# Chunk 0's 2 KB rows of q and k, dealt to partitions by sixteenth of the chunk instead of by head

## The chip, the core and the metric

The kernel runs on one core of a Trainium2 chip. The metric is device time in microseconds (us) of one execution: 240.31 us, the median of three runs from 240.06 to 241.03. The execution that was profiled took 239.83 us.

## What is computed

A retention layer with a recurrent state per head, followed by a gated feed-forward layer. Sizes: 4 batches, 8 heads, 768 positions, head width 64; feed-forward width 1536.

```python
gamma = 1.0 - 2.0 ** (-5.0 - np.arange(H))
for t in range(S):
    state = gamma * state + np.einsum('bhd,bhe->bhde', k[:, :, t], v[:, :, t])
    y[:, :, t] = np.einsum('bhd,bhde->bhe', q[:, :, t], state) / np.sqrt(D)
x = y.transpose(0, 2, 1, 3).reshape(B * S, H * D)
xn = x / np.sqrt(np.mean(x * x, -1, keepdims=True) + 1e-6) * rms_g
g = xn @ w_gate
out = (g / (1 + np.exp(-g)) * (xn @ w_val)) @ w_out
```

All inputs and the output are float32 in HBM, q, k and v laid out as batch, head, position, width.

## The kernel before, in words

The recurrence is computed by chunks: 768 positions are 6 chunks (c) of 128, and each chunk has 4 batches (b). For one (c, b) the steps are: load q, k and v; make them bfloat16; turn q and k so that the width is on partitions (`qT`, `kT`); scores `a = kT qT` for all heads (L382); scores times a decay mask (`am`, L405); `y = am v`, plus the state's part for c > 0 (L420, L424); mean square (`S`, L448, ScalarE), its inverse root (`R`, L458 and L460, GpSimd), normalised rows `xn` (`N`, L472, VectorE), turned to `xnT`; and the update of the state (`K`, `U`, `B`). Then the feed-forward layer for the 512 rows of a chunk: `g` and `v` matmuls over 12 blocks of the width (L538), SiLU (`s`, L548), product (`h`, L556), and the matmul with `w_out` (`d`, L563).

The order of all work is written out by hand in the string `ORDER`: each word is one step, done by one function, and each engine executes its own instructions in that order. A word such as `Lk.0.2@S>iota` reads: load k, chunk 0, batch 2, issued by SyncE (S), after the step `iota`. `Tk.0.3/5` is the turning of k of batch 3 on TensorE into PSUM bank 5; `Ek.0.3@D` is the copy of that bank to SBUF on VectorE; `Ck.0.2@D` is a cast to bfloat16 on VectorE. `H.14` and `hot.3` are matmuls on a tile of ones whose result nobody reads.

Chunk 0's q and k are loaded in a way of their own. A row of the load is 8 consecutive positions of one head, 8 x 64 float32 = 2 KB. There are 8 heads x 16 groups of 8 positions = 128 such rows, one for each partition. The access pattern is made on L139, and the load is issued on L291:

```python
by8 = {n: x.rearrange("b h (c s j) d -> c b h s (j d)", s=C // NJ, j=NJ)[0] for n, x in (("q", q), ("k", k))}
i = done[n, c, b] = e.dma_start(out=flat(x), in_=by8[n][b])
```

So partition 16 h + s holds positions 8 s to 8 s + 7 of head h. Three of these eight loads (k of batches 0, 3 and 2, in this order) are issued by SyncE in float32 and cast on chip (`Ck`). Five (q of batches 2 and 1, k of batch 1, q of batches 0 and 3, in this order) are issued by GpSimd, which lets the transfer write bfloat16: 2 KB rows are read and 1 KB rows written. All other loads of q, k and v have a partition per position, with 256-byte runs of the heads (L293).

`T` turns a loaded tile: for each of the 8 positions j of a row and each parity i of the head it makes one matmul of the tile's slice (128 partitions x 64) with 64 columns of the identity matrix, picked by `pick` (L345) so that the columns are head pair, then group s. In this kernel these columns are 4 runs of 16 neighbouring columns. That is 16 matmuls for one tile. `E` copies the bank to SBUF and puts the positions in order.

VectorE's order at the start is: constants, `Ck.0.2`, `Ck.0.3`, then the copies `Eq.0.2`, `Ek.0.3`, `Ek.0.2`, `Eq.0.0`, then `D.0.2` (L506) and the masked scores (L405). TensorE's is: `H.14`, `Tk.0.3`, `Tq.0.2`, `hot.3`, `Tq.0.1`, `Tk.0.2`, `Tk.0.0`, `H.1`, `Tq.0.0`, `Tk.0.1`, then the scores. GpSimd issues, in order, the five loads above, v of batches 0, 2 and 1, k of chunk 1 batch 1, `wv` columns 0 to 255, v of batch 3, three loads of `wg` and one of `wv`, and k of chunk 1 batch 0; its ninth and later loads each wait until the load eight before has landed. Only after them in its queue come the `R` steps and then the next weight load, `wv.4.6`.

Of the kernel before, what the change touches and what calls it, by code (L numbers as in the profile page):

```python
# [103 lines left out]
def kernel(  # L104
# [15 lines left out]
    C = 128  # L120
    NCH = S // C
    NHP = H // 2
# [13 lines left out]
    rows = {n: s.rearrange("b h (c p) d -> b c p h d", p=C) for n, s in (("q", q), ("k", k), ("v", v))}  # L136

    NJ = 8
    by8 = {n: x.rearrange("b h (c s j) d -> c b h s (j d)", s=C // NJ, j=NJ)[0] for n, x in (("q", q), ("k", k))}  # L139

    DVE, ACT, POOL, SP = nc.vector, nc.scalar, nc.gpsimd, nc.sync
    ENG = {"D": DVE, "A": ACT, "P": POOL, "S": SP}
# [5 lines left out]
    def flat(x):  # L148
        return x.rearrange("p h d -> p (h d)")
# [24 lines left out]
    ident = const.tile([128, 128], BF16, name="ident")  # L174
# [22 lines left out]
    def bank(i, shape, dtype, name):  # L197
        return psum.tile(shape, dtype, name=name, tag=f"bank{i}")
# [142 lines left out]
    def T(n, bk, c, b):  # L341
        u = t[c, b]
        if c == 0:
            u[n + "P"] = p = bank(bk[0], [128, NHP, NJ, C // NJ], F32, "t_ps")
            pick = ident.rearrange("p (hp i s) -> p i hp s", i=2, hp=NHP)  # L345
            for j in range(NJ):
                for i in range(2):
                    nc.tensor.matmul(p[i * 64:i * 64 + 64, :, j, :], u[n + "b"][:, j, :], pick[:, i],  # L348
                                     start=True, stop=True)
            return  # L350
        u[n + "P"] = bank(bk[0], [128, NHP, 128], BF16, "t_ps")
        for hp in range(NHP):
            nc.tensor.transpose(u[n + "P"][:, hp, :], flat(u[n + "b"])[:, hp * 128:(hp + 1) * 128], ident)  # L353
# [14 lines left out]
    for n in "qk":  # L368
        F["T" + n] = lambda e, bk, c, b, n=n: T(n, bk, c, b)
        F["E" + n] = lambda e, bk, c, b, n=n: E(n, e, c, b)  # L370
        F["t" + n] = lambda e, bk, c, b, n=n: tr(n, c, b)
# [253 lines left out]
```

## Time and profile before

| what | value |
|---|---|
| profiled execution | 239.83 us |
| its span, first to last instruction | 238.1 us |
| outside the span | 1.7 us |
| TensorE busy | 225.5 us, 95% of the span |
| VectorE, ScalarE, GpSimd busy | 55%, 41%, 38% |
| mean granted TensorE clock | 0.993 |
| DMA over the span | 34.27 MB, mean 144 GB/s |
| the three k loads by SyncE issued | 0.79 to 2.9 us |
| the five 2 KB-row loads by GpSimd issued | 2.08 to 5.23 us |
| first cast of a loaded tile on VectorE | 10.35 us |

The profile gives, among others: the busy share of each engine in slices of the span; the chain of work that ended last, followed back from the last instruction, with its releasers; the waits; the instructions in order of time; and, for chosen stretches, busy time, the granted TensorE clock, the DMA share (mean number of packets in flight per DMA engine, of 16) and the rate. The trace also has a record of each DMA packet (start, length, bytes) and of each count that a load adds to its semaphore when a part of it has landed; a load has landed with the sixteenth count.

### The profile page before, as it was taken

How to read it: one execution, taken by the hardware profiler on the slowest of the kernel's cores; microseconds unless marked ns; L12 is line 12 of the kernel's file. 1: busy time of each engine (PE TensorE's matmuls, PEld its weight loads, DVE VectorE, ACT ScalarE, POOL GpSimd, SP SyncE). 2: the span in 40 equal slices, each digit the busy share in tenths (PEclk: the TensorE clock that was granted, in tenths of full speed). 3: DMA queues.
4: the chain of work that ended last, by engine and by line, in shares of the span. 5: the costliest groups of instructions: out<-in, count | busy, mean ns of one | idle time of the engine just before them, and what ended most of it. 6: DMA issues, size and time to landing. Idle time of an engine off the chain costs nothing.

```text
span 238.1 us, 4684 instructions
## 1 busy us (share of the span) xinstructions
PE 225.5 (95%) x1782; PEld 121.0 (51%) x1807; DVE 131.2 (55%) x234; ACT 97.1 (41%) x234; POOL 90.3 (38%) x164
## 2 busy tenths in 40 slices
PE   8099999999989999999999999999999999999995
PEld 2066785545544466544554445545454444444453
DVE  3179647874686769445575428693675441432300
ACT  6158565633444274064432044423176321233021
POOL 8584898271350615426137242266504000000000
PEclk9979999999999999999999999999999999999999
DMA  3999599999948796799999999899503302001123
GB/s 99 182 159 161 55 178 220 206 201 214 194 94 188 155 225 145 174 227 191 203 237 179 197 222 181 170 214 149 150 3 82 75 23 78 10 0 44 48 106 116
DMA packets 101233, 34.27 MB, mean 144 GB/s; under 512 B 89945, under 2 KB 97625, under 8 KB 101210
## 3 DMA queue, kind: packets, MB, share of 16 engines
q1 hardware_dynamic: 80186, 25.97, 54.4%
q0 software_dynamic: 21024, 8.00, 27.4%
q8 instruction: 14, 0.23, 0.4%
q14 instruction: 9, 0.07, 0.1%
HBM read 28.31 MB, written 6.29 MB: 145 GB/s over the span
## 4 chain that ended last, share of the span: by engine, by line
PE 84%; DVE 5%; DMA 3%; POOL 3%; issue 2%; ACT 1%; SPq 1%; POOLq 0%; ACTq 0%
PE o_ps L563 25%; PE v_ps L538 24%; PE g_ps L538 23%; DMA kf<-in_k_dram 3%; PE a_ps L382 2%; PE kv_ps L515 2%; PE y_ps L420 2%; DVE am L405 2%; PE y_ps L424 1%; PE t_ps L348 1%; PE o_ps L585 1%; POOL rstd L460 1%; PE t_ps L353 1%; DVE kb L146 1%; PE xt_ps L485 1%
## 5 line engine op out<-in xcount | busy, mean ns | idle before, releaser
L556 DVE TENSOR_TENSOR hT<-sg,v_ps 128x512 bf16<-128x512 bf16 (+2 forms) x76 | 48.0, 656 | 51.5 <-PE v_ps L538 34.1
L538 PE MATMUL v_ps<-xnT,wv_b 128*128 128x512 bf16 (+2 forms) x335 | 71.3, 343 | 1.3 <-DVE hT L556 1.0
L538 PE MATMUL g_ps<-xnT,wg_b 128*128 128x512 bf16 (+2 forms) x337 | 70.9, 344 | 0.5 <-issue 0.2
L548 ACT ACTIVATE sg<-g_ps 128x512 bf16<-128x512 f32 (+2 forms) x76 | 42.1, 574 | 66.3 <-PE g_ps L538 64.3
L563 PE MATMUL o_ps<-wo_b,hT 128*128 128x512 bf16 x267 | 62.2, 379 | 0.5
L538 PEld LDWEIGHTS <-wv_b 128*128 128x128 bf16 x344 | 30.2, 98 | 29.1 <-issue 1.2
L538 PEld LDWEIGHTS <-wg_b 128*128 128x128 bf16 x344 | 30.3, 98 | 28.7
L563 PEld LDWEIGHTS <-hT 128*128 128x128 bf16 x276 | 26.2, 98 | 29.3 <-DVE hT L556 0.3
L405 DVE TENSOR_TENSOR am<-a_ps,causal 128x512 bf16<-128x512 f32 x40 | 25.7, 684 | 7.0 <-PE a_ps L382 7.0
L320 POOL TENSOR_TENSOR qb<-qf,ydec 128x512 bf16<-128x512 f32 x13 | 14.2, 1093 | 24.2 <-DMA qf<-in_q_dram 24.2
L146 ACT COPY o_sb<-o_ps 128x512 f32<-128x512 f32 (+2 forms) x17 | 9.2, 549 | 34.2 <-PE o_ps L563 32.7
L530 POOL CAST st_b<-st_f 64x256 bf16<-64x256 f32 x40 | 17.6, 440 | 8.6 <-PE y_ps L424 4.6
L146 DVE COPY o_sb<-o_ps 128x512 f32<-128x512 f32 (+1 forms) x9 | 5.8, 650 | 22.4 <-PE o_ps L563 12.3
L458 POOL TENSOR_SCALAR ms<-ssq 128x1 f32<-128x1 f32 x24 | 4.6, 192 | 31.1 <-ACT xsq L448 30.2
L460 POOL TENSOR_TENSOR rstd<-ms,mhalf 128x1 f32<-128x1 f32 x24 | 13.6, 567 | 2.0
L448 ACT ACTIVATE xsq<-y_ps 128x512 f32<-128x512 f32 x14 | 8.4, 598 | 10.7 <-PE y_ps L424 9.2
L523 DVE TENSOR_TENSOR st_f<-st_f,kv_ps 128x512 f32<-128x512 f32 x16 | 10.7, 682 | 3.3 <-POOL st_b L530 2.0
L472 DVE SCALAR_TENSOR_TENSOR xn<-y_ps,rstd,g_bc 128x512 bf16<-128x512 f32 x14 | 10.4, 747 | 1.8 <-POOL rstd L460 1.6
L337 ACT ACTIVATE vp<-vf,vdec 128x64 bf16<-128x64 f32 x40 | 10.1, 338 | 1.3 <-DMA vf<-in_v_dram 1.3
L339 POOL TENSOR_TENSOR vp<-vf,vdec 128x512 bf16<-128x512 f32 x8 | 8.8, 1100 | 3.3 <-DMA vf<-in_v_dram 3.2
L231 PE MATMUL hot_ps<-one 128*128 128x512 bf16 x23 | 7.6, 472 | 1.1 <-DVE one L153 1.1
L420 PEld LDWEIGHTS <-am 128*128 128x128 bf16 x144 | 6.4, 98 | 4.0 <-DVE am L405 1.0
(97 smaller groups left out, 187.3 us busy)
## 6 DMA issues: line engine op xcount, KB each, us to landing
out_dram<-o_sb SPq DMA_DIRECT2D x23, 256.0 KB, 2.6
kf<-in_k_dram SPq DMA_DIRECT2D x19, 256.0 KB, 4.4
qf<-in_q_dram SPq DMA_DIRECT2D x16, 256.0 KB, 3.7
vf<-in_v_dram SPq DMA_DIRECT2D x16, 256.0 KB, 4.0
wo_b<-in_moe_w_out_dram POOLq DMA_DIRECT2D x3, 512.0 KB, 13.0
qb<-in_q_dram POOLq DMA_DIRECT2D x8, 128.0 KB, 7.2
vf<-in_v_dram POOLq DMA_DIRECT2D x4, 256.0 KB, 8.5
wv_b<-in_moe_w_val_dram POOLq DMA_DIRECT2D x3, 256.0 KB, 6.1
```

The costliest lines, as they stand in the source:

```text
L146: (e.copy if e is ACT else e.tensor_copy)(out, in_)
L320: e.tensor_tensor(out=u["qb"], in0=u["qf"], in1=ydec[:, c, :, None].to_broadcast([128, H, D]), op=ALU.mult)
L405: DVE.tensor_tensor(out=u["am"][:, i], in0=u["a"][i], in1=m, op=ALU.mult)
L420: nc.tensor.matmul(y[:, h, :], u["am"][:, h % 2, h // 2, :], u["vp"][:, h, :], start=h == 0, stop=c == 0 and h == H - 1, skip_group_check= ...
L460: POOL.tensor_tensor(out=u["rstd"], in0=ms, in1=mhalf, op=ALU.pow)
L472: DVE.scalar_tensor_tensor(out=u["xn"], in0=flat(u.get("x", u["y"])), scalar=u["rstd"], in1=g_bc, op0=ALU.mult, op1=ALU.mult)
L523: DVE.tensor_tensor(out=st_f[b], in0=st_f[b], in1=t[c, b]["kv"], op=ALU.add)
L530: POOL.tensor_copy(st_b[b][r, :, i * 64:i * 64 + 64], st_f[b][r, :, i * 64:i * 64 + 64])
L538: nc.tensor.matmul(p[:, (n - n0) * m:(n - n0 + 1) * m], W[w][0][:, s, n * 128:(n + 1) * 128], xnT[c][:, s, b0 * C:b1 * C], start=s == 0, s ...
L548: ACT.activation(sg[:, :cols], done["wg", c, n0, b0][:, :cols], AF.Silu)
L556: DVE.tensor_tensor(out=hT[c][:, n0:n1, b0 * C:b1 * C], in0=sg, in1=p, op=ALU.mult)
L563: nc.tensor.matmul(o_ps[c, b], hT[c][:, n, b * C:(b + 1) * C], wo_b[:, n, :], start=n == 0, stop=n == NFF - 1)
```

## The change

The sixteenth of the chunk, s, becomes the outer dimension of the DRAM side of these eight loads, and the head the inner one. Partition 8 s + h then holds positions 8 s to 8 s + 7 of head h. Rows are 2 KB as before and there are 128 of them; neighbouring partitions now read rows one head apart, 768 x 64 x 4 bytes = 192 KB, where they read neighbouring rows before. `pick` follows: its 64 columns are now single columns, 8 apart, in place of runs of 16.

```diff
-    by8 = {n: x.rearrange("b h (c s j) d -> c b h s (j d)", s=C // NJ, j=NJ)[0] for n, x in (("q", q), ("k", k))}
+    by8 = {n: x.rearrange("b h (c s j) d -> c b s h (j d)", s=C // NJ, j=NJ)[0] for n, x in (("q", q), ("k", k))}
...
-            pick = ident.rearrange("p (hp i s) -> p i hp s", i=2, hp=NHP)
+            pick = ident.rearrange("p (s hp i) -> p i hp s", i=2, hp=NHP)
```

The instructions of every engine, their number and their order are the same in both kernels.

## Prediction

> **What bounds the kernel.** I read the page first: TensorE is busy 95% of the span, so time can only be saved where it is not. The 40 slices of busy tenths show where: the second (6 to 12 us) has a 0, all others but the last have 8 or 9.
>
> ```profile
> PE   8099999999989999999999999999999999999995
> ...
> PEclk9979999999999999999999999999999999999999
> ```
>
> Right behind it, in the third slice, the granted clock is 0.7, the only one below 0.9. Next the chain that ended last, in order of time.
>
> ```profile
> 2.29 8.03 DMA kf<-in_k_dram
> 10.32 0.02 issue
> 10.35 1.16 DVE kb L146 x2
> 11.50 0.04 issue
> 11.55 1.07 PE t_ps L348 x32
> ...
> 14.94 0.39 PE t_ps L348 x16
> 15.33 0.02 issue
> 15.35 0.60 DVE qT L146
> 15.95 0.05 issue
> 16.00 0.69 DVE kd L506
> 16.70 2.99 DVE am L405 x5
> ```
>
> The end hangs on a transfer: SyncE's third k load (batch 2) lands at 10.32 us; then two casts, the turning of q and k, and VectorE's queue, which is busy without a gap over 0.4 us from 15.35 (`Eq.0.0`) to 24.8 us. From there to the end the chain is almost all TensorE: no DMA stands in it again. So a microsecond won before 15.35 is a microsecond won at the end, unless a transfer becomes late behind it.
>
> Then the stretches around these loads (the last columns are granted clock, DMA share of 16 engines, GB/s).
>
> ```profile
> 2.50:3.50 1.00, 1.00 (x4) 0.32 (x3) 0.74 (x3) 0.99 (x2) 1.00 (x2) 1.00 0.37 102
> 3.50:4.50 1.00, 1.00 (x4) 0.30 (x3) 0.00 (x0) 1.00 (x4) 1.00 (x3) 1.00 0.59 203
> 5.50:7.00 1.50, 0.46 (x3) 0.00 (x0) 0.00 (x0) 1.24 (x5) 1.50 (x2) 1.00 1.01 186
> 18.00:21.00 3.00, 2.94 (x54) 1.94 (x55) 3.00 (x6) 2.13 (x6) 0.96 (x3) 1.00 1.45 196
> 24.00:27.00 3.00, 2.83 (x45) 2.40 (x42) 1.99 (x6) 1.45 (x4) 2.02 (x6) 1.00 0.00 0
> ```
>
> While only SyncE's loads move (3.5 to 4.5), the share is about a half. By the packet records 50 packets of 2 KB start in each half microsecond and each takes 84 ns: 50 x 84 / 500 = 8.4 in flight. The counts say the same: eight of a load's sixteen come at once (first load: by 1.95 us, before its first packet at 2.30), eight with the data (4.44 to 4.91). Loads with 128 rows outermost (v of batch 0) bring all sixteen with their data. So a load whose DRAM side has 8 as outer dimension is worked by eight engines, 16 packets each. GpSimd's loads are also dealt to eight, and by their counts alternate between the two halves: q.0.2, k.0.1 and q.0.3 share the half of SyncE's three loads, and land at 10.11, 11.25 and 12.62.
>
> **The change: transfers.** With 16 as outer dimension I take it that each load runs on sixteen engines, 8 packets each. SyncE's three loads are then 24 packets per engine in place of 48. Of them 3 go in the slow first 0.7 us (26 packets on eight engines from 2.3 to 3.0 in the record), 21 at 84 ns = 1.76: last packet done at 2.3 + 0.7 + 1.76 = 4.76. GpSimd's first load joins at 4.0 to 4.9 and may put 3 of its packets (98 ns) between: 5.1. The last count came 0.35 to 0.8 us behind the first load's last packet: I take 0.4. Landing 5.5, not 10.32: **-4.8 us**.
>
> GpSimd's issues stay at 2.08 to 5.23 (0.6 each). Its loads now need 8 x 98 ns = 0.8 us each. From about 4.9: q.0.2 lands at 6.2, q.0.1 7.0, k.0.1 7.7, q.0.0 8.5, q.0.3 9.3; then v of batches 0, 2, 1, at 0.85 apart as in the counts of before: 10.2, 11.0, 11.9 (13.49, 14.33, 15.17 before). Its ninth load waits for q.0.2's landing (2.4 us of idle, at 10.39); that is gone, since q.0.2 lands while it still issues (to 7.97). The nine loads from k.1.1 to k.1.0 took 9.2 us after v.0.1 (15.17 to 24.39): now to about 21.
>
> **The change: the turning.** From VectorE's first cast to `Eq.0.0` it was 15.35 - 10.35 = 5.0 us: 1.2 for the casts, 3.8 for six tiles' turning, of which 3.2 at clock 0.50. TensorE then had been idle from 5.96 to 11.54. Now the casts end at 6.7 and it is idle for 0.7 us, so I take the full clock. A tile's 16 matmuls then take 0.27 (14.87 to 15.14) in place of 0.44 (11.55 to 11.99):
>
> ```profile
> 11.55 0.64 PE L348 MATMUL t_ps<-ident,kb 128*64 128x64 bf16 x16 [5.59 <-DVE kb L146]
> 11.99 0.62 PE L348 MATMUL t_ps<-ident,qb 128*64 128x64 bf16 x16
> ...
> 14.87 0.44 PE L348 MATMUL t_ps<-ident,qb 128*64 128x64 bf16 x16
> 15.14 0.42 PE L348 MATMUL t_ps<-ident,kb 128*64 128x64 bf16 x16
> ```
>
> Six tiles (1.65) and the two blocks of filler matmuls (0.55) end at 6.7 + 2.2, with 0.15 until the copy; VectorE's three copies before `Eq.0.0` (0.6 each) begin 0.7 after the first tile: 6.7 + 0.7 + 1.8 = 9.2. Both give `Eq.0.0` at about 9.2, 3.7 after the first cast: **-1.3 us**. Sum -6.1.
>
> The new `pick` reads single columns 8 apart. No row before reads a moving tile with gaps. Bounds: 0 (the rows above, same matmul, nearest), and 2.5 times a tile's time, from the farthest matmul row, float32 columns (L275, two in 1.12 us, 0.56 each against 0.22 for 512 bfloat16 columns): 6 x (0.68 - 0.27), about +2.4. A gain has no source. I take +0.1, near the first: its copies leave little cover.
>
> **What is late next.** Needed against landing, after: q.0.1 7.5 against 7.0; q.0.0 8.75 against 8.5; v.0.2 (first y, 2.6 after `Eq.0.0`) 11.8 against 11.0; the first `wg` (23.9 before, 17.8 now) against 16.2. All hold, q.0.0 barely. The next weight load stands behind GpSimd's `R` of batch 3, so its issue (25.80) moves with the chain to 19.7 and its packets (27.4) to 21.3, just when k.1.0's are through: the empty 24 to 27 us shown above is used up, and more than about -6.1 would not be followed by the weights. These are nearly late already: `wg.6.9`, `wv.6.9` and `wg.9.12` land 1.0, 0.6 and 0.8 us before their first use at 36.6, 39.9 and 42.9. So a chain that gains 6.0 has weights that gain about 6.0, and the slack stays.
>
> **Forecast:** 239.83 - 6.0 = 233.8 for a profiled execution; the median of the runs is 0.5 above that execution: 234.3, and 232.9 to 235.0 for this case. Chance 0.60.
>
> **Rivals.**
> (a) Transfers scale less than I take, or GpSimd's q.0.0 arrives late and TensorE waits. The fastest half microsecond with 2 KB packets in it (6.5 to 7.0) moved 230 GB/s; at that rate 786 KB take 3.4 us, the landing is at 6.8, gain 4.8: 235.5. For it: no row has sixteen engines on 2 KB packets. Against: 18 to 21 us wrote 196 GB/s in bfloat16, which is 390 read. 0.16.
> (b) The gapped columns cost. At twice the time per tile (0.54) six tiles and the fillers take 3.8, and `Eq.0.0` is at 10.65, 1.5 later: gain 4.6, 235.7; at 2.5 times (0.68) it is 2.3 later: 236.5. [...] No run here shows it yet. 0.13.
> (c) The loads stay on eight engines: 240.3. Against it are the sixteen counts with data of loads with 128 outermost. [...] 0.05.
> (d) Slower: each engine now jumps 192 KB from row to row. If a jump cost what the first ten packets did (336 ns against 84), the 56 packets per engine up to q.0.0 would take 18.8 us: landing 2.5 + 18.8 + 0.4 = 21.7. q.0.0 may land at 14.9 without loss (`Eq.0.0` at 15.35), so 6.8 are lost: 247. It decides from 0.21 us per packet. Against it: eight engines on eight heads, 192 KB apart, already run at 84 ns. 0.06.
>
> **How the numbers follow.** Faster by over 0.5% (1.2 us, about what a measurement of this kernel can tell): forecast, (a) and (b), 0.89; within: (c), 0.05; slower: (d), 0.06. The range reaches from the forecast's lower end to a microsecond past (b)'s upper end, for (a) and (b) together: 233.0 to 237.5; it leaves out (c), (d) and a little of the forecast.
>
> **What would show it.** The third k load landing near 5.5 with a DMA share near 1 by 3.5 to 4.5; all sixteen counts with data; VectorE's first cast near 5.5, `Eq.0.0` near 9.2; clock 1.0 through the turning, 16 matmuls in 0.27; GpSimd without the 2.4 us wait; `wv.4.6` issued near 19.7; no weight wait of TensorE at 30 to 37 us. Wrong if packets grow well over 100 ns, if a tile's turning takes over 0.4 at full clock, or if the chain after 24 us shows a DMA.

## The result and the profile after

The changed kernel is slower, by less than a per cent: 242.77 us (median of 14 runs, 240.65 to 245.46) against 240.65 us (14 runs, 240.06 to 241.31). The ratio is 1.007, 95% interval 1.0044 to 1.0096; the three slowest runs of the changed kernel, with a mean granted clock of 0.965, are left out of it. The prediction was 234.3 us, range 233.0 to 237.5. The profiled execution took 241.65 us, its span 239.9, 1.8 more than before.

The busy slices of the page, of the changed kernel. The idle stretch of the second slice (the 0 before) is a 5 now: TensorE starts earlier. But the granted clock, the last row, is lower there (6, where it was 9).

```profile
PE   8599999999989999999999999999999999999994
...
PEclk9679999999999999999999999999999999999999
```

The chain that ended last, in order of time (start, length, what):

```profile
2.15 5.56 DMA kf<-in_k_dram
7.71 0.02 issue
7.73 1.19 DVE kb L146 x2
8.93 0.04 issue
8.97 2.05 PE t_ps L348 x32
11.02 0.43 PE hot_ps L225 x3
11.46 2.92 PE t_ps L348 x47
14.38 0.54 PE hot_ps L231
14.92 1.97 PE t_ps L348 x31
16.89 0.34 PE t_ps L500 x4
...
17.33 0.69 DVE kd L506
18.02 1.21 DVE am L405 x2
```

The third k load lands at 7.71, not 10.32. Behind it, the turning of six tiles, from the first matmul to `Eq.0.0`, has grown from 3.8 to 7.0 us (8.97 to 16.00). The stretches of before, again (granted clock, DMA share, GB/s last):

```profile
2.50:3.50 1.00, 1.00 (x4) 0.32 (x3) 0.74 (x3) 0.99 (x2) 1.00 (x3) 1.00 0.87 293
3.50:4.50 1.00, 1.00 (x4) 0.30 (x3) 0.00 (x0) 1.00 (x4) 1.00 (x3) 1.00 1.04 237
```

The DMA share is about 1 in place of 0.59: I read that as sixteen engines at work, and all sixteen counts of the first load come with its data (3.69 to 4.37 us). But the rate in the second line is only 237 GB/s. And the tiles' turning, TensorE in order of time (start, length of the group, shape, count):

```profile
8.97 1.12 PE L348 MATMUL t_ps<-ident,kb 128*64 128x64 bf16 x16 [2.93 <-DVE kb L146]
9.90 1.12 PE L348 MATMUL t_ps<-ident,qb 128*64 128x64 bf16 x16
...
14.85 1.11 PE L348 MATMUL t_ps<-ident,qb 128*64 128x64 bf16 x16
15.78 1.11 PE L348 MATMUL t_ps<-ident,kb 128*64 128x64 bf16 x16
```

From one tile's start to the next it is 0.93 us, where it was 0.44 at half clock and 0.27 at full. The last pair runs at 0.93 although the clock is back at full from 14.9 (TensorE busy, granted clock, DMA share, GB/s):

```profile
8.10:14.80 6.70, 5.83 (x84) 0.50 1.97 165
15.00:17.00 2.00, 2.00 (x36) 1.00 1.52 199
```

**Where the 1.8 us of the span come from.** Against before: first cast 2.6 earlier (7.73, 10.35); from it to `Eq.0.0` 8.3 us instead of 5.0, +3.3; the seventh tile, before the scores, +0.7 (the product `kd` of step `D.0.2` starts at 17.33 against 16.00, so 1.3 late, where `Eq.0.0` at 16.00 is 0.65 late); the eighth tile, ahead of the last batch, the rest. The first `g` matmul (L538) starts at 25.86, not 23.93; from there both kernels do the same.

### The profile page after: what moved, and what is told of

It reads as the page before. It is cut to its first block, busy times and chain, and to the rows that moved or that the text cites. A ratio compares the mean times of both kernels' runs of the same rounds, so it can differ in the third digit from the quotient of the medians.

```text
span 239.9 us, 4684 instructions
## 1 busy us (share of the span) xinstructions
PE 230.0 (96%) x1782; PEld 125.0 (52%) x1807; DVE 131.5 (55%) x234; ACT 97.0 (40%) x234; POOL 89.9 (37%) x164
## 3 DMA queue, kind: packets, MB, share of 16 engines
q1 hardware_dynamic: 80210, 25.97, 54.5%
## 4 chain that ended last, share of the span: by engine, by line
PE 86%; DVE 3%; POOL 3%; issue 2%; DMA 2%; ACT 1%; SPq 1%; POOLq 0%; ACTq 0%; DVEq 0%
PE o_ps L563 24%; PE v_ps L538 24%; PE g_ps L538 23%; PE t_ps L348 3%; DMA kf<-in_k_dram 2%; PE a_ps L382 2%; PE y_ps L420 2%; PE kv_ps L515 2%; PE y_ps L424 1%; PE o_ps L585 1%; POOL rstd L460 1%; ACT xsq L448 1%; PE hot_ps L231 1%; DVE kb L146 1%; PE t_ps L353 1%
## 5 line engine op out<-in xcount | busy, mean ns | idle before, releaser
L538 PE MATMUL v_ps<-xnT,wv_b 128*128 128x512 bf16 (+2 forms) x335 | 71.3, 343 | 1.3 <-DVE hT L556 1.0
L538 PE MATMUL g_ps<-xnT,wg_b 128*128 128x512 bf16 (+2 forms) x337 | 70.9, 344 | 0.5 <-issue 0.2
L538 PEld LDWEIGHTS <-wg_b 128*128 128x128 bf16 x344 | 30.4, 98 | 28.7
L538 PEld LDWEIGHTS <-wv_b 128*128 128x128 bf16 x344 | 30.2, 98 | 29.1 <-issue 1.2
```

Of the source, the lines that this page charges most:

```text
L538: nc.tensor.matmul(p[:, (n - n0) * m:(n - n0 + 1) * m], W[w][0][:, s, n * 128:(n + 1) * 128], xnT[c][:, s, b0 * C:b1 * C], start=s == 0, s ...
```

## The experiments

Theory A: the gapped columns of `pick` are what costs, the loads gain. (`pick` is the operand of 64 columns in the turning's matmuls, called the moving one below; the other, the tile's 128 x 64 slice, is loaded ahead of it: the rows `PEld L348 LDWEIGHTS <-kb` of 128*64, with a median of 157 ns before and 152 after.) Rivals: B, it is the loads (their 192 KB jumps, or their writes slowing TensorE's reads); C, it is the half clock. Times stand beside runs of the kernel before on the same chip: median 240.38 us (11 runs) for e1 to e4, 240.47 (12 runs) for e5 to e8, a single run of 241.57 for e9 to e11.

**1. Runs again, by a permuted copy of the identity (e1).**

```diff
+        DVE.tensor_copy(idp.rearrange("p (hp i s) -> p hp i s", i=2, hp=NHP), ident.rearrange("p (s hp i) -> p hp i s", i=2, hp=NHP))
...
-            pick = ident.rearrange("p (s hp i) -> p i hp s", i=2, hp=NHP)
+            pick = idp.rearrange("p (hp i s) -> p i hp s", i=2, hp=NHP)
```

> The changed loads, but the identity is copied once on VectorE into another tile in an order in which the turning's 64 columns are again runs of 16. Theory A (the gapped columns cost, the loads themselves gain): 16 matmuls of a tile go back from 0.93 us to 0.27 (full clock) or 0.43 (half), the third k load still lands near 7.7 us, the copy Eq.0.0 starts at 11.3 to 12.8 us in place of 15.35 before, and the time is 236.5 to 238 us. Theory B (it is the loads: jumps of 192 KB, or their writes into SBUF that slow TensorE's reads): a tile's turning stays near 0.9 us and the time near 242. Theory C (the half clock is the cause): 0.43 per tile, no better than before, 239 to 241.

Measured: 237.26 us (6 runs, 236.34 to 238.57), ratio 0.9875 (0.9842 to 0.9908). Third k load at 7.82, `Eq.0.0` at 12.55, and tiles again 0.28 us apart at full clock (9.07 and 9.35) and 0.44 at half (11.87 and 12.31):

```profile
9.07 0.44 PE L350 MATMUL t_ps<-idp,kb 128*64 128x64 bf16 x16 [2.03 <-DVE kb L146]
9.35 0.42 PE L350 MATMUL t_ps<-idp,qb 128*64 128x64 bf16 x16
```

Same loads, other columns: B falls.

**2. The gapped columns with the loads of before (e2).** L139 as before; a permuted copy of the identity puts the same columns 8 apart.

> The loads of before, with the gapped columns of the change (the identity copied once into an order in which the same columns lie 8 apart). Theory A: a tile takes 0.93 us as in the changed kernel, though the load is the old one; TensorE starts at 11.5 as before, so against the changed kernel the start is 2.6 us later: 244 to 246 us. Theory B: 0.27 to 0.43 per tile and the time of before, 240.5. Theory C: between, since the clock is as in before.

Measured: 244.44 us (4 runs, 242.71 to 245.29), ratio 1.0184 (1.0143 to 1.0226). TensorE of this kernel:

```profile
10.53 1.12 PE L350 MATMUL t_ps<-idp,kb 128*64 128x64 bf16 x16 [3.31 <-DVE kb L146]
11.46 1.12 PE L350 MATMUL t_ps<-idp,qb 128*64 128x64 bf16 x16
```

The tile takes 0.93 with the old loads too. The first tile did not start at 11.5, as expected, but at 10.53, since the third k load landed at 9.63 in this execution. So A stands with both signs: the change is a gain of the loads (-1.2%, e1) and a larger loss of the columns (+1.8%, e2), and the two together give the +0.7% of the change within their intervals.

**3. Which gap costs (e3, e4, e10, and e5 below).** A permuted copy of the identity with columns 2, 4 and 16 apart. Of each edit the line of `pick` is shown; e4 also splits the head pairs of the matmul's output in two to match.

```diff
-            pick = ident.rearrange("p (s hp i) -> p i hp s", i=2, hp=NHP)
+            pick = idp.rearrange("p (hp s i) -> p i hp s", i=2, hp=NHP)          # e3: 2 apart
+            pick = idp.rearrange("p (a s b i) -> p i a b s", a=2, b=2, i=2)      # e4: 4 apart
+            pick = idp[:, :, 0].rearrange("p s hp i -> p i hp s")                # e10: 16 apart
```

> Changed loads, columns 2 apart (4 bytes). [...]

> Changed loads, columns 4 apart (8 bytes). [...]

> Changed loads, columns 16 apart (32 bytes), from a copy of the identity with empty places between. Theory A2 (cost per 16-byte line): 64 lines as with a gap of 8, so 54 to 56 ns per matmul. If the cost grows with the distance: about 110 ns.

Measured from the starts of a tile's matmuls, in ns per matmul of 64 columns, for tiles that lie whole within one clock. A line here is 8 neighbouring bfloat16 columns, 16 bytes; the second column counts how often the 64 columns, in the order of the access pattern, enter another one:

| columns apart | 16-byte lines | full clock | half clock |
|---|---|---|---|
| runs of 16 (before, e1) | 8 | 15.0 to 16.4 | 24.9 to 26.7 |
| 2 (e3) | 16 | 15.0 to 16.6 | 24.9 to 26.4 |
| 4 (e4) | 32 | 27.3 | 28.4 to 28.7 |
| 8 (after, e2, e8) | 64 | 53.3 to 54.7 | 54.5 to 56.2 |
| 16 (e10) | 64 | 54.3 to 55.3 | 55.5 |

The times, of a single execution each: 236.34, 238.24 and 242.11 us. Columns 2 apart keep the pace of runs, so a gap as such does not cost. The time at full clock doubles from 4 to 8 apart (27.3, 53.3 to 54.7) and does not grow from 8 to 16 (54.3 to 55.3): it goes with the number of lines entered, about 0.86 ns for each (55 / 64, 28 / 32), at either clock, and shows where that exceeds the matmul's own pace (15.0 to 16.4 ns at full clock and 24.9 to 26.7 at half, with runs). The unit of 16 bytes is read from these rows alone: of the gaps that were run, 8 columns is the first beyond which the time grows no more. Two columns to a line (e4) already cost 27.3 at full clock against 16.4.

**4. The same columns read line by line (e5), and with a busy TensorE ahead (e6).**

```diff
-            u[n + "P"] = p = bank(bk[0], [128, NHP, NJ, C // NJ], F32, "t_ps")
-            pick = ident.rearrange("p (s hp i) -> p i hp s", i=2, hp=NHP)
+            u[n + "P"] = p = bank(bk[0], [128, NJ, C // NJ, NHP], F32, "t_ps")
+            pick = ident.rearrange("p (s hp i) -> p i s hp", i=2, hp=NHP)
...
-                    nc.tensor.matmul(p[i * 64:i * 64 + 64, :, j, :], u[n + "b"][:, j, :], pick[:, i],
+                    nc.tensor.matmul(p[i * 64:i * 64 + 64, j], u[n + "b"][:, j, :], pick[:, i],
...
-u[n + "P"].rearrange("p hp j s -> p hp s j")
+u[n + "P"].rearrange("p j s hp -> p hp s j")
```

e6 has also `H.24` for `H.14` at the head of `ORDER`.

> Changed loads; the 64 columns are the same ones of the same identity, but read with the head pair innermost (4 columns 2 apart, then the next 16 bytes), and the bank is laid out to match; no copy of the identity. Theory A2 (a matmul takes 0.86 ns per 16-byte line of its moving columns, at either clock, or its own pace if that is longer): 16 lines, so 16.4 ns per matmul at full and 25 at half clock, as with runs; 236.5 to 237.7 us. Rival: the steps of the order matter, not the lines, and the tile stays between 28 and 55 ns per matmul: 238 to 242 us.

> The kernel before this one with ten more filler matmuls ahead (24 for 14), so that TensorE is idle for under 1 us before the first tile. If the half clock is what the idle stretch costs: clock 1.0 through the turning, 16.4 ns per matmul for all eight tiles, Eq.0.0 1.0 us earlier (11.5 to 11.8), and 0.5 to 1.0 us less in time. If the clock falls anyway or another wait takes its place: the time of the kernel without them.

Measured: e5 237.02 us (6 runs, 236.52 to 237.56), ratio 0.9858 (0.9827 to 0.9888); e6 236.39 (6 runs, 235.37 to 236.58), ratio 0.9827 (0.9798 to 0.9855). In e5 the clock was at half for the first seven tiles (24.9 to 26.4 ns per matmul). In e6 it stayed full, as TensorE in order of time shows, 0.28 from tile to tile:

```profile
9.31 0.44 PE L348 MATMUL t_ps<-ident,kb 128*64 128x64 bf16 x16
9.59 0.42 PE L348 MATMUL t_ps<-ident,qb 128*64 128x64 bf16 x16
...
11.41 0.44 PE L348 MATMUL t_ps<-ident,qb 128*64 128x64 bf16 x16
11.69 0.42 PE L348 MATMUL t_ps<-ident,kb 128*64 128x64 bf16 x16
```

`Eq.0.0` starts at 11.90 in e6, 13.35 in e5. Both start their first tile at 9.3, so the 1.45 us between them are the turning's, at full clock and at half; 1.0 was expected. The medians differ by 0.6 us, as expected, but the intervals of the ratios overlap. The ten fillers end 0.6 us after the first tile was ready (casts done at 8.7), so a few less might do better; that was not run.

**5. The changed kernel with a busy TensorE ahead (e8).** Only `H.24` for `H.14`.

> The changed kernel with ten more filler matmuls ahead. The gapped tiles took 54 to 55 ns per matmul at both clocks, so theory A2 says the tiles stay at 0.93 us. If the half clock makes the rest of the loss and the scatter of the changed kernel (241 to 245 us, longer with a lower mean clock): 240.5 to 241.5 with little scatter. If the clock has no part: 242 to 243, scatter as before.

Measured: 242.85 us (5 runs, 241.63 to 243.79), ratio 1.0099 (1.0064 to 1.0135): no gain, tiles as slow as ever. The first tile of e8, and its stretches (TensorE busy, granted clock, DMA share, GB/s):

```profile
8.78 1.10 PE L348 MATMUL t_ps<-ident,kb 128*64 128x64 bf16 x16 [0.57 <-DVE kb L146]
...
8.80:11.40 2.60, 2.60 (x43) 1.00 2.21 160
11.80:14.80 3.00, 3.00 (x45) 0.50 1.95 175
```

TensorE is busy without a gap in both stretches, at 53.5 to 54.8 ns per matmul. The fillers did not keep the clock: TensorE was idle for 0.57 us ahead of the first tile, and the clock was at half from 11.5 to 14.9. But the two tiles that lie in the full clock of the first stretch are as slow as those in the second, so C falls as the cause of the slow tiles. What the half clock adds to the time of the changed kernel is not separated by this run.

**6. Why the third k load lands at 7.7 and not 5.5 (e7, e9, e11).** e7 holds GpSimd's loads until SyncE's three have landed; e9 and e11 are e7 with other rows read, so q and k are not the reference's.

```diff
+        if (n, c, b) == ("q", 0, 2):
+            after(i, ("k", 0, 2))
...
-    by8 = {n: x.rearrange("b h (c s j) d -> c b s h (j d)", s=C // NJ, j=NJ)[0] for n, x in (("q", q), ("k", k))}
+    by8 = {n: x.rearrange("b h s d -> b (h s d)")[:, :16 * 4160].rearrange("b (s r) -> b s r", s=16)[:, :, :4096].rearrange("b s (h f) -> b s h f", h=H) ...}   # e9
+    by8 = {n: x.rearrange("b h s d -> b (h s d)")[:, :C * DM].rearrange("b (s h f) -> b s h f", s=C // NJ, h=H) ...}   # e11
```

> The changed kernel, with GpSimd's loads held until SyncE's third k load has landed. If sharing the engines with GpSimd's loads is what made that load land at 7.7: 2 KB packets of 84 to 97 ns throughout and a landing at 5.0 to 5.4. If the jumps of 192 KB or the sixteen engines' own limit are: packets of 120 ns and more in the second half, a landing at 6.3 or later. The time is longer either way, 243 to 246, since q comes later.

> The kernel with SyncE's k loads alone first, but the eight loads read other rows: still 16 groups of eight 2 KB rows, the eight now next to each other in HBM (2 KB apart, not 192 KB), the groups 16.25 KB apart; q and k are not the reference's. SyncE's second and third load took 1.05 us each there (packets of 138 to 144 ns). Theory J (the jumps of 192 KB cost): packets back to 84 to 97 ns, 0.65 us per load, the third landing at 5.2 to 5.6. Theory W (the writing side limits sixteen engines that write 2 KB into 8 neighbouring partitions each): packets stay near 140 ns, landing at 6.4 to 6.7.

> The same, with one contiguous stretch of 256 KB per load, so that both sides have 128 rows as outer dimension; q and k are not the reference's. Theory J: as the kernel with 16 near groups, 0.65 us per load. Theory W: faster than 16 groups only if 128 rows are dealt to the engines in another order than neighbouring eights; then 0.65 us here and 1.05 there.

Measured, in a single execution each: the three loads landed at 4.47, 5.55, 6.56 in e7 (241.76 us, less than the 243 to 246 expected); at 4.45, 5.50, 6.47 in e9 (244.28, with the clock at half from 9.6 to 26.7); at 3.47, 4.09, 5.53 in e11 (240.64). The stretches of e7 and e9, one line each, and two of e11:

```profile
3.50:4.50 1.00, 1.00 (x4) 0.40 (x3) 0.00 (x0) 1.00 (x4) 0.00 (x0) 1.00 1.09 250
```

```profile
3.50:4.50 1.00, 1.00 (x4) 0.30 (x3) 0.00 (x0) 1.00 (x4) 0.00 (x0) 1.00 1.07 266
```

```profile
2.50:3.50 1.00, 1.00 (x4) 0.32 (x3) 0.74 (x3) 0.99 (x2) 0.00 (x0) 1.00 1.00 381
3.50:4.50 1.00, 1.00 (x5) 0.35 (x4) 0.00 (x0) 1.00 (x4) 0.00 (x0) 1.00 0.75 168
```

Sharing is half of the answer: alone, the load lands 1.15 earlier than in the changed kernel, not 2.2. The jumps are none of it: rows 2 KB apart (e9) are as slow as rows 192 KB apart (e7), 0.97 to 1.08 us per load. The other half is not settled. The second load of e11, 128 rows in one stretch, lands 0.62 behind the first, and the stretch in which it moves has 381 GB/s; that points to the outer dimension of 16, but no run here shows how it would slow the packets, so theory W stays open. Two things in the records stand against taking even the outer dimension as the cause. In e7 the first load has the same one, and its last 64 packets took 85 ns each; the slow ones, 132 to 144 ns, begin with the second load. And the third load of e11 was held up by a stretch of slow packets (173 ns on average from 3.5 to 4.0), whose cause is open, and landed 1.44 behind the second, so that the two together took 2.06 us in e11 and 2.09 in e7.

## Why the prediction was wrong

- **The step that failed** is "Bounds: 0 ... and 2.5 times a tile's time ... I take +0.1, near the first". A tile takes 0.93 us, 3.4 times the 0.27, outside both bounds. Six tiles cost 4.0 us more than assumed, and the two behind them about another 1.3. The upper bound came from a row with 2.5 times the time for another reason (float32 columns without gaps, 0.56 us against 0.22), so it bounded nothing here; no row of before had gaps. Rival (b) named the place and had 0.13. The changed kernel, e2 and e8 show that 8 columns apart is not free (53.3 to 56.2 ns), and e3 and e4 that 4 apart already costs at full clock (27.3) and 2 does not (15.0 to 16.6).
- **Landing 5.5**, rival (a): mis-sized. It was 7.71: 1.05 us for the second and the third load on sixteen engines (e7) where I took 0.67 (the 84 ns of eight engines, kept for sixteen), 0.8 from the last packet to the last count (5.75 to 6.56 in e7) where I took 0.4, and 1.15 for sharing with GpSimd where I took 0.3.
- **Eight engines before, sixteen after**: right, as far as the counts and the share tell (all sixteen counts of the first load at 3.69 to 4.37 us, with its data, where eight stood by 1.95 before; share 1.04 against 0.59). No row names an engine. Rival (c) falls. Rival (d), the jumps, falls by e9.
- **Full clock for the turning**: wrong. TensorE was idle for 2.9 us, not 0.7, as the load landed later, and the clock was at half from 8.1 to 14.9. For the pace of gapped tiles that changed next to nothing (53.3 to 54.7 ns at full clock, 54.5 to 56.2 at half); for tiles read line by line, e5 against e6, it is the 1.45 us by which `Eq.0.0` moves.
- **The 2.4 us wait of GpSimd** went, to 0.24 (next load issued at 7.82, not 10.39), as forecast.
- **"More than about -6.1 would not be followed by the weights"**: they came close sooner. In e6, where the chain gains 3.45 us up to the first `g` (20.48 against 23.93), `wg.6.9`, `wv.6.9` and `wg.9.12` land 0.26, 0.09 and 0.17 us before use, against 1.0, 0.6 and 0.8. The end gains about 3.3 in that execution (236.58 against 239.83).

With columns that use their lines up, the loads give 3.1 us (e1), 3.5 (e5) and, with the clock at full, 4.1 (e6), against the 6.0 forecast. In e6 the third k load landed at 7.39, 1.9 behind the 5.5 of the forecast, which is about what is missing; that it is the landing is argued from this size, not shown. So the forecast's mechanism was there, with about two thirds of its size, and the term that it put at +0.1 turned the sign.

## What to carry to other kernels

When a layout is changed to please the DMA, look at every access pattern that must follow it, and at the innermost step of a moving operand first: with bfloat16, count the 16-byte lines that the columns enter in their order, and compare 0.86 ns per line with the matmul's pace (both as measured here, for 64 columns: 54 ns with 64 lines against 15.0 to 16.4 with runs, at full clock). If no row of the profile shows such a pattern, its cost is unbounded until one is run, and a large share of the chance belongs to it. Here the same elements could be read in an order that uses each line up (e5), at the pace of runs (24.9 to 26.4 ns at half clock).

## What the runs showed of the hardware

- A moving operand of 64 bfloat16 columns cost about 0.86 ns per 16-byte line that it entered, at either granted clock (64 lines: 54 ns at 1.0, 55 at 0.5; 32 lines: 27.3 and 28.4 to 28.7). With 16 lines or fewer nothing of it showed behind the matmul's own pace (15.0 to 16.6 ns at 1.0, 24.9 to 26.7 at 0.5).
- With gapped tiles and fillers back to back the clock was at half until 17.3 in e2 (TensorE busy from 10.53) and from 9.4 to 12.9 in e10 (busy from 9.06). What brought it back to full is open.
- In single executions, with GpSimd's loads held back, 2 KB float32 rows moved at 250 GB/s (e7) and 266 (e9) from 3.5 to 4.5 us with 16 groups of eight rows, and in e11, with 128 rows, at 381 from 2.5 to 3.5 and 168 from 3.5 to 4.5; in the kernel before, with 8 as the outer dimension, it was 203 from 3.5 to 4.5.
